# Token rows and gate products from bfloat16 thirds in place of fp32 matmuls

## The chip, the cores and the metric

One core of one Trainium2 chip. The metric is the device time of one execution in microseconds (us). A block is 128 tokens; most token chunks have four.

## The reference, cut to what matters

An input of 4 x 3072 x 256 goes through a two-dimensional Fourier transform (real part kept), a gated channel mix, and a mixture of 8 experts that gives every token to one expert as long as the expert has room.

```python
x = fft(fft(x, axis=1), axis=2).real                     # 4 x 3072 x 256
k = np.maximum(xk @ w_k, 0.0);  v = k * k @ w_v          # xk, xr: x mixed with the token before
r = 1.0 / (1.0 + np.exp(-(xr @ w_r)))
x = (r * v).reshape(12288, 256)                          # gated outputs, one row a token
logits = x @ w_gate                                      # 8 gate products a token
expert_idx = np.argmax(logits, axis=1)
...
# a token whose expert still has a free slot (384 each) goes through w1, relu, w2,
# times its softmax weight; all other rows of the output are zero
```

The choice of the expert is by the largest of eight products, so these are needed nearly exactly.

## The kernel before, in words

**Stages.** Up to 36 us: constants, weights cut into two fp32r halves, the first transform. From then to 470 us: token chunks of 512 (chunk 12 has 384, chunk 13 has 256). In this stage the Fourier transforms of the later inputs run as "units" placed between the matmuls of a chunk (`plan`, `lay`, L1047 to L1063). From 470 on: eight experts, each with two matmul stages, and the scatter of their results.

**A chunk (`chunk`, L647).** The channels lie on the 128 lanes and the tokens run along the free axis. Eight steps f: `mm_k` makes a hidden tile (six matmuls of 512 columns), ScalarE takes relu and square, `halves` (L538) lets VectorE cut it into two fp32r halves kh and kl, and `mm_v` uses them LAG = 3 steps later (six matmuls). So the last three `mm_v` of a chunk fall into the first three steps of the next one. In step 2 of chunk i the sums `pv` of chunk i - 1 are complete: `gated` (L556) multiplies them with the sigmoid on VectorE, into the tile rT, and the bank `pv` is free for `mm_v(i, 0)`. `mm_r(i)` follows (twelve matmuls). In steps 4 and 5 `to_rows` (L563) turns the gated outputs of chunk i - 1 into rows. For each block two matmuls, one per half of the 256 channels, have rT's block as the stationary operand and `gm` as the moving one: an identity of 128 columns with 8 gate columns beside it. They write 136 columns each, overlapping by 8, into 264 columns of one bank: 128 outputs, 8 gate products summed over both halves, 128 outputs. ScalarE copies them into `rows` (L576). One fp32 matmul runs as two passes, each with a weight load of its own.

**The choice.** `pick` (L578) finds the largest product on VectorE (L590 to L597) and leaves a one-hot tile `oh`. `route` (L600, step 6) counts tokens per expert with small bf16 matmuls on `oh` (L605, L609). `slots` and `place` make the slot numbers, `send` scatters the rows with an indirect transfer from GpSimd (L186) to `disp` in memory, whose row width is `RW`. The experts later read `disp` (`load_slots`, L1200) and turn rows back with `ident` (`turn`, L1217).

**The last chunk.** After chunk 13 `finish` (L693) does the same without a following chunk around it: `gated`, `to_rows`, `pick`, `route`, then `slots` and a flag which decides whether more blocks of tokens are needed. In this run they are not, so 14 chunks with 53 blocks are done.

**Order.** The schedule is manual: every engine executes in the order of the program text, and `later`/`tick` move a VectorE or ScalarE step behind the next matmul group. PSUM banks: three `pk` for hidden tiles, three `pm` for transforms, rows and routing, two `pv`. `gm` is filled by four transfers on SyncE's queue (L1016, L1017) at about 31 to 34 us, ahead of the loads of `w_v`; `ident` comes by ScalarE's queue (L930).

```python
if f == LAG - 1 and prev is not None:
    gated(prev)
if f == (LAG - 1 if i else LAG + 1):
    mm_r(i)
    tick()
```

Of the kernel before, what the change touches and what calls it, by code (L numbers as in the profile page):

```python
# [10 lines left out]
F32 = mybir.dt.float32  # L11
F32R = mybir.dt.float32r
BF16 = mybir.dt.bfloat16
I32 = mybir.dt.int32
AF = mybir.ActivationFunctionType
ALU = mybir.AluOpType
# [4 lines left out]
P = 128  # L21
# [11 lines left out]
CH = 512  # L33
# [6 lines left out]
GATE = 128  # L40
# [67 lines left out]
def fourier_channel_mix_moe(  # L108
# [6 lines left out]
    nc = tc.nc  # L115
    x = ins["x"]
    B, S, D = x.shape
    DFF = ins["w_k"].shape[1]
    E, _, F2 = ins["w1"].shape
    N = B * S  # L120
    KD = D // P
    KF = DFF // P
    KF2 = F2 // P
    RW = D + E + 1
    ST = cap // P
    NSLOT = E * cap
    TT = CH // P
    assert S == P * NC and D == 2 * P and cap % P == 0 and B == 4 and E == 8
    YC = (slice(0, P), slice(P + E, D + E))
    LC = slice(GATE, GATE + E)  # L130
    chunks = [(b, s, w) for b in range(B) for s, w in cut(b, S)]
    NCH = len(chunks)

    cst = ctx.enter_context(tc.tile_pool(name="cst", bufs=1))
# [3 lines left out]

    disp = drp.tile([NSLOT, RW], F32, name="disp")

    ident = cst.tile([P, P], F32, name="ident")
    flag = cst.tile([P, 1], I32, name="flag")
    slot = cst.tile([P, TT], I32, name="slot")
    rows_of = cst.tile([P, TT, RW], F32, name="rows")
    mix = ExitStack()
    psv = mix.enter_context(tc.tile_pool(name="psv", bufs=1, space=PSUM))
    wts = mix.enter_context(tc.tile_pool(name="wts", bufs=1))
# [3 lines left out]
    neg_i = wts.tile([P, P], F32R, name="neg_i")  # L151
    ulp_i, negulp_i = (wts.tile([P, P], BF16, name=f"ulp{k}") for k in range(2))
    ones = wts.tile([P, P], BF16, name="ones")
    gm = wts.tile([P, KD, P + E], F32, name="gm")
    w8 = wts.tile([P, TT, E], F32, name="w8")
    lim = wts.tile([P, TT, E], F32, name="lim")
    base = wts.tile([P, E], F32, name="base")
# [15 lines left out]
    mir = wts.tile([P, (len(CSTEPS) - 1) * B], I32, name="mir")  # L173
    blank = wts.tile([P, RW], F32, name="blank")

# [333 lines left out]
    live = {}  # L509
# [46 lines left out]
    def gated(i, step=None):  # L556
        rT, v = live[i, "r"], live.pop((i, "v"))
        w = chunks[i][2]
        for t in range(0, w, step or w):
            ts = slice(t, t + (step or w))  # L560
            nc.vector.tensor_tensor(rT[:, :, ts], v[:, :, ts], rT[:, :, ts], op=ALU.mult)  # L561

    def to_rows(i, ts):  # L563

        yT = live[i, "r"]
        if ts[0] == 0:
            live[i, "rows"] = early["rows"] if i == stop1 - 2 else rows_of
        rows = live[i, "rows"]
        for t in ts:
            ps = psm.tile([P, CH], F32, name="pm")  # L570
            for d in range(KD):
                nc.tensor.matmul(
                    ps[:, P * d:P * (d + 1) + E], yT[:, d, t * P:(t + 1) * P], gm[:, d],
                    start=(d == 0), stop=(d == KD - 1), skip_group_check=True,
                )
            nc.scalar.copy(rows[:, t, :D + E], ps[:, :D + E])  # L576

    def pick(i, clear=False):  # L578

        b, s, w = chunks[i]  # L580
        n = w // P
        rows = live[i, "rows"]
        nc.gpsimd.iota(
            rows[:, :n, RW - 1:].bitcast(I32), pattern=[[P, n], [0, 1]], base=b * S + s, channel_multiplier=1
        )
        if clear:
            nc.gpsimd.drain()
        lg = rows[:, :n, LC]
        mx = mp.tile([P, TT, 1], F32, name="mx")[:, :n]
        nc.vector.tensor_reduce(mx, lg, op=ALU.max, axis=AX.X)  # L590
        nc.vector.tensor_tensor(lg, lg, mx.to_broadcast([P, n, E]), op=ALU.subtract)
        key = mp.tile([P, TT, E], F32, name="key")[:, :n]
        nc.vector.scalar_tensor_tensor(key, lg, 0.0, w8[:, :n], op0=ALU.is_ge, op1=ALU.mult)
        mx2 = mp.tile([P, TT, 1], F32, name="mx2")[:, :n]
        nc.vector.tensor_reduce(mx2, key, op=ALU.max, axis=AX.X)
        oh = mp.tile([P, TT, E], BF16, name="oh")[:, :n]
        nc.vector.tensor_tensor(oh, key, mx2.to_broadcast([P, n, E]), op=ALU.is_equal)  # L597
        live[i, "oh"] = oh
# [48 lines left out]
    def chunk(i, prev, fill, nxt, mixes, also=()):  # L647


        also = dict(also)  # L650
        n = chunks[prev][2] // P if prev is not None else 0
        for f in range(KF):
            if f in also:
                also[f]()
            if f == 0 and (i, 1, 0) not in xm:
                mix_part(i, 0)
                mix_part(i, 1)
                settle()
            if f == (0 if i else 2) and (i, 0, 0) not in xm:
                for d in range(KD):  # L660
                    mix_part(i, 2 + d)
                if i and prev is None:
                    settle()
            mm_k(i, f)
            tick()
            if f >= LAG:
                mm_v(i, f - LAG)
                tick()
            elif prev is not None:
                mm_v(prev, KF - LAG + f)  # L670
                tick()
            if f == LAG - 1 and prev is not None:
                gated(prev)
            if f == (LAG - 1 if i else LAG + 1):
                mm_r(i)
                tick()
            if prev is not None:
                if f == LAG + 1:
                    to_rows(prev, range(0, min(2, n)))
                if f == LAG + 2:  # L680
                    if n > 2:
                        to_rows(prev, range(2, n))
                    later(1, lambda: pick(prev, True))
                if f == LAG + 3:
                    route(prev)
                    later(1, lambda: (slots(prev), place(prev), send(prev)))
            if nxt is not None and f in mixes:
                mix_part(nxt, mixes.index(f))
            for u in fill[f]:
                u()  # L690
                tick()

    def finish(i, before=lambda: None, between=lambda: None, after=lambda: None):  # L693
# [18 lines left out]
        "x": [[t.rearrange("p t s -> p (t s)")[:, cap * k:cap * (k + 1)] for t in fbuf["G"][0]] for k in range(KD)],  # L712
        "d": spare1[:, :ST * RW].rearrange("p (t w) -> p t w", w=RW),
        "rows": spare1[:, ST * RW:2 * ST * RW].rearrange("p (t w) -> p t w", w=RW),
        "count": spare1[:, 2 * ST * RW:2 * ST * RW + cap],
# [15 lines left out]
    def early_turn(k, last):  # L731
        ps = bank()
        for t in range(ST):
            nc.tensor.matmul(
                ps[:, t * P:(t + 1) * P], early["d"][:, t, YC[k]], ident, start=(t == 0),
                stop=(last and t == ST - 1), skip_group_check=True,
# [38 lines left out]
    def early_parts(i, step):  # L775
        for k, (h, l) in enumerate(early_room(i)[1]):
            v = live[i, "rows"][:, :h.shape[1], YC[k]]
            if step == 0:
# [116 lines left out]
    with tc.manual_schedule():  # L895
        with tc.tile_pool(name="stg", bufs=2) as stg:
# [116 lines left out]
            pw["r"][1]()  # L1013
            pw[0, 1][2]()
            for d in range(KD):
                nc.sync.dma_start(gm[:, d, P * (1 - d):P * (1 - d) + E], ins["w_gate"][d * P:(d + 1) * P])  # L1016
                nc.sync.dma_start(gm[:, d, E * d:E * d + P], ins["c_ident"])  # L1017
        mp = mix.enter_context(tc.tile_pool(name="mp", bufs=1))
        late_buffers(mp)
        vp = ExitStack()  # L1020
# [282 lines left out]
        for e in range(1, E + 1):  # L1303
            for f in range(KF2):
                if e < E:
                    up(e, f)
                t = f // 2 - 1 if e > 1 else f
# [43 lines left out]
```

## Time and profile before

| | |
|---|---|
| three timed runs | 622.03, 625.03, 629.35 us; median 625.03 |
| the profiled execution | 620.86 us, its span 619.1 us |
| mean granted TensorE clock | 0.989 |
| TensorE (PE) busy | 589.2 us, 95% of the span |
| VectorE (DVE) busy | 409.0 us, 66% |
| ScalarE (ACT) busy | 361.7 us, 58% |
| GpSimd (POOL) busy | 125.4 us, 20% |

Times in the rows are us from the start of the span unless marked ns. PE is a matmul, PEld a weight load, SPq the issue of a transfer on SyncE. [...] In a timeline a row merges equal instructions that follow each other (x8); brackets give the idle time of the engine before them and what ended it.

### The profile page before, as it was taken

How to read it: one execution, taken by the hardware profiler on the slowest of the kernel's cores; microseconds unless marked ns; L12 is line 12 of the kernel's file. 1: busy time of each engine (PE TensorE's matmuls, PEld its weight loads, DVE VectorE, ACT ScalarE, POOL GpSimd, SP SyncE). 2: the span in 40 equal slices, each digit the busy share in tenths (PEclk: the TensorE clock that was granted, in tenths of full speed). 3: DMA queues.
4: the chain of work that ended last, by engine and by line, in shares of the span. 5: the costliest groups of instructions: out<-in, count | busy, mean ns of one | idle time of the engine just before them, and what ended most of it. 6: DMA issues, size and time to landing. Idle time of an engine off the chain costs nothing. (4 is left out here: it accounts for less than half of the span.)

```text
span 619.1 us, 9641 instructions
## 1 busy us (share of the span) xinstructions
PE 589.2 (95%) x3365; PEld 506.7 (82%) x3367; DVE 409.0 (66%) x924; ACT 361.7 (58%) x710; POOL 125.4 (20%) x181
## 2 busy tenths in 40 slices
PE   6888988999999999999999999999997999999996
PEld 3474667888888788887888888889996999999996
DVE  5667896988665756799756565756764685665540
ACT  2556765666655566666655565565644675565551
POOL 7300052503020303050202030302221111111112
PEclk7999999999999999999999999999998999999999
DMA  8699342614242500152313052000023875555401
GB/s 275 228 341 318 127 152 86 215 43 138 54 144 76 166 0 22 34 187 87 126 46 104 14 186 89 6 2 3 3 63 92 303 214 162 177 152 163 124 26 35
DMA packets 55579, 74.02 MB, mean 120 GB/s; under 512 B 6288, under 2 KB 41469, under 8 KB 55522
## 3 DMA queue, kind: packets, MB, share of 16 engines
q1 hardware_dynamic: 48178, 58.35, 29.8%
q0 software_dynamic: 5936, 13.37, 6.5%
q10 hardware_dynamic: 1408, 1.60, 0.8%
q8 instruction: 29, 0.48, 0.3%
q14 instruction: 28, 0.23, 0.1%
HBM read 43.31 MB, written 33.91 MB: 125 GB/s over the span
## 5 line engine op out<-in xcount | busy, mean ns | idle before, releaser
L504 PE MATMUL pk<-x,wk 128*128 128x512 f32 (+2 forms) x672 | 171.1, 389 | 4.3 <-DVE x L218 1.7
L504 PEld LDWEIGHTS pk<-x,wk 128*128 128x128 f32 x672 | 118.7, 189 | 27.6 <-DVE x L218 2.6
L504 PE MATMUL pv<-kh,wv 128*128 128x512 f32 (+2 forms) x448 | 134.2, 381 | 2.3 <-DVE rT L561 1.4
L535 ACT ACTIVATE rk<-pk 128x512 f32<-128x512 f32 (+2 forms) x112 | 64.4, 575 | 85.0 <-PE pk L504 82.6
L186 POOL DMA_INDIRECT disp<-rows,slot x50 | 53.8, 1076 | 255.5 <-ACT tmp L494 64.4
L539 DVE CAST kh<-rk 128x512 fp32r<-128x512 f32 (+2 forms) x106 | 44.4, 419 | 85.9 <-ACT rk L536 85.5
L504 PEld LDWEIGHTS pv<-kh,wv 128*128 128x128 f32 x448 | 82.4, 188 | 19.8 <-DVE rT L561 2.3
L504 PE MATMUL pv<-kl,wv 128*128 128x512 f32 (+2 forms) x224 | 85.3, 381 | 0.0
L540 DVE TENSOR_TENSOR kl<-rk,kh 128x512 fp32r<-128x512 f32 (+2 forms) x112 | 74.5, 665 | 9.9 <-ACT kh L539 4.0
L1250 PE MATMUL pd<-w,h 128*128 128x256 f32 x576 | 72.5, 282 | 0.0
L1250 PEld LDWEIGHTS pd<-w,h 128*128 128x128 f32 x576 | 71.6, 191 | 0.0
L536 ACT ACTIVATE rk<-rk 128x512 f32<-128x512 f32 (+2 forms) x112 | 68.2, 609 | 3.6
L1198 DVE TENSOR_TENSOR w<-raw,w 128x512 fp32r<-128x512 f32 x60 | 41.0, 687 | 39.7 <-ACT w L1197 39.7
L504 PEld LDWEIGHTS pv<-kl,wv 128*128 128x128 f32 x224 | 42.1, 188 | 8.1
L186 POOL DMA_INDIRECT out<-res,ids x24 | 24.0, 998 | 117.5 <-ACT res L1259 117.2
L1241 DVE SCALAR_TENSOR_TENSOR h<-pk,h 128x384 fp32r<-128x384 f32 x64 | 35.3, 552 | 14.4 <-ACT h L1240 14.4
L1259 ACT ACTIVATE res<-pd,g 128x256 f32<-128x256 f32 x24 | 11.3, 476 | 53.6 <-PE pd L1250 52.1
L217 ACT CAST x<-tmp 128x512 fp32r<-128x512 f32 (+2 forms) x56 | 32.8, 587 | 14.2 <-DVE tmp L495 14.0
L504 PE MATMUL pk<-x,wr 128*128 128x512 f32 (+2 forms) x168 | 39.1, 382 | 0.0
L1197 ACT CAST w<-raw 128x512 fp32r<-128x512 f32 x60 | 36.6, 614 | 0.0
L218 DVE TENSOR_TENSOR x<-tmp,x 128x512 fp32r<-128x512 f32 (+2 forms) x56 | 36.5, 655 | 0.1
L504 PEld LDWEIGHTS pk<-x,wr 128*128 128x128 f32 x168 | 30.7, 188 | 6.3
(214 smaller groups left out, 861.6 us busy)
## 6 DMA issues: line engine op xcount, KB each, us to landing
raw<-in_w SPq DMA_DIRECT2D x60, 256.0 KB
out<-blank SPq DMA_DIRECT2D x24, 512.0 KB
xin<-in_x SPq DMA_DIRECT2D x15, 256.0 KB
tin<-fd SPq DMA_DIRECT2D x18, 208.0 KB
fd<-f SPq DMA_DIRECT2D x14, 256.0 KB
disp<-blank SPq DMA_DIRECT2D x6, 530.0 KB
d<-disp SPq DMA_DIRECT2D x8, 397.5 KB
rawv<-in_w_v SPq DMA_DIRECT2D x4, 512.0 KB
```

The source lines that it names most:

```text
L186: i = nc.gpsimd.indirect_dma_start(out=dst, out_offset=bass.IndirectOffsetOnAxis(ap=idx, axis=0), in_=src, in_offset=None, bounds_check=la ...
L217: nc.scalar.copy(hl[0], src)
L218: later(n, lambda: nc.vector.tensor_tensor(hl[1], src, hl[0].bitcast(F32), op=ALU.subtract))
L504: nc.tensor.matmul(ps, w[a][:, k, m0:m0 + P], xs[c], start=(first and n == 0), stop=(last and n == 2),)
L535: nc.scalar.activation(r, ps, AF.Relu)
L536: nc.scalar.activation(r, r, AF.Square)
L539: nc.vector.tensor_copy(kh, r) if i or f > 5 else nc.scalar.copy(kh, r)
L540: nc.vector.tensor_tensor(kl, r, kh.bitcast(F32), op=ALU.subtract)
L1197: nc.scalar.copy(h, r)
L1198: nc.vector.tensor_tensor(l, r, h.bitcast(F32), op=ALU.subtract)
L1241: nc.vector.scalar_tensor_tensor(hl, ps, 0.0, hh.bitcast(F32), op0=ALU.max, op1=ALU.subtract)
L1250: nc.tensor.matmul(ps, hs[a][:, f, t * P:(t + 1) * P], w[c][:, f], start=(f == 0 and n == 0), stop=(f == KF2 - 1 and n == 2),)
```

## The change

`thirds` cuts the gated output y of a chunk into three bf16 parts that add up to it exactly: the upper half word of y, the upper half word of the rest r, and what is then left. `gm` becomes bf16 and holds the gate weights cut in the same way, beside the identity. Each block and half gets one matmul per part of y in place of one fp32 matmul. The first part meets three parts of the gate weights (24 columns beside the identity), the second two, the third one, so the products stand in three groups of 8 columns, and `pick` adds these up. The moving operand is `gm`; the stationary ones are the parts of y, each spaced by one half word in an fp32 tile. `finish` doesn't call `thirds`: there the fp32 `gw`, whose added 16 columns are zero, is used as before, with 152 columns. `RW` grows from 265 to 281. `ident` is now a part of `gw`. The parts of the gate weights are made on GpSimd, once.

```diff
--- before.py
+++ after.py
@@ -121,12 +121,12 @@
     KD = D // P
     KF = DFF // P
     KF2 = F2 // P
-    RW = D + E + 1
+    RW = D + 3 * E + 1
     ST = cap // P
     NSLOT = E * cap
     TT = CH // P
     assert S == P * NC and D == 2 * P and cap % P == 0 and B == 4 and E == 8
-    YC = (slice(0, P), slice(P + E, D + E))
+    YC = (slice(0, P), slice(P + 3 * E, D + 3 * E))
     LC = slice(GATE, GATE + E)
     chunks = [(b, s, w) for b in range(B) for s, w in cut(b, S)]
     NCH = len(chunks)
@@ -138,7 +138,8 @@
 
     disp = drp.tile([NSLOT, RW], F32, name="disp")
 
-    ident = cst.tile([P, P], F32, name="ident")
+    gw = cst.tile([P, KD, P + 3 * E], F32, name="gw")
+    ident = gw[:, 0, :P]
     flag = cst.tile([P, 1], I32, name="flag")
     slot = cst.tile([P, TT], I32, name="slot")
     rows_of = cst.tile([P, TT, RW], F32, name="rows")
@@ -151,7 +152,8 @@
     neg_i = wts.tile([P, P], F32R, name="neg_i")
     ulp_i, negulp_i = (wts.tile([P, P], BF16, name=f"ulp{k}") for k in range(2))
     ones = wts.tile([P, P], BF16, name="ones")
-    gm = wts.tile([P, KD, P + E], F32, name="gm")
+    gm = wts.tile([P, KD, P + 3 * E], BF16, name="gm")
+    gf = wts.tile([P, KD, E], F32, name="gf")
     w8 = wts.tile([P, TT, E], F32, name="w8")
     lim = wts.tile([P, TT, E], F32, name="lim")
     base = wts.tile([P, E], F32, name="base")
@@ -560,20 +562,35 @@
             ts = slice(t, t + (step or w))
             nc.vector.tensor_tensor(rT[:, :, ts], v[:, :, ts], rT[:, :, ts], op=ALU.mult)
 
+    def upper(t):
+        return t.bitcast(BF16)[..., 1::2]
+
+    def thirds(i):
+        w = chunks[i][2]
+        y = live[i, "r"]
+        r = mp.tile([P, KD, CH], F32, name="yr")[:, :, :w]
+        low = r.bitcast(BF16)[..., 0::2]
+        nc.vector.tensor_tensor(r, y, upper(y), op=ALU.subtract)
+        nc.vector.tensor_tensor(low, r, upper(r), op=ALU.subtract)
+        live[i, "y"] = [upper(y), upper(r), low]
+
     def to_rows(i, ts):
 
-        yT = live[i, "r"]
+        ys = live.pop((i, "y")) if ts[-1] == chunks[i][2] // P - 1 and (i, "y") in live else live.get((i, "y"))
+        ys = [(live[i, "r"], gw)] if ys is None else [(y, gm) for y in ys]
         if ts[0] == 0:
             live[i, "rows"] = early["rows"] if i == stop1 - 2 else rows_of
         rows = live[i, "rows"]
         for t in ts:
             ps = psm.tile([P, CH], F32, name="pm")
             for d in range(KD):
-                nc.tensor.matmul(
-                    ps[:, P * d:P * (d + 1) + E], yT[:, d, t * P:(t + 1) * P], gm[:, d],
-                    start=(d == 0), stop=(d == KD - 1), skip_group_check=True,
-                )
-            nc.scalar.copy(rows[:, t, :D + E], ps[:, :D + E])
+                for k, (y, g) in enumerate(ys):
+                    c = slice(E * k, P + 3 * E) if d else slice(0, P + E * (3 - k))
+                    nc.tensor.matmul(
+                        ps[:, P * d + c.start:P * d + c.stop], y[:, d, t * P:(t + 1) * P], g[:, d, c],
+                        start=(d == k == 0), stop=(d == KD - 1 and k == len(ys) - 1), skip_group_check=True,
+                    )
+            nc.scalar.copy(rows[:, t, :RW - 1], ps[:, :RW - 1])
 
     def pick(i, clear=False):
 
@@ -586,6 +603,8 @@
         if clear:
             nc.gpsimd.drain()
         lg = rows[:, :n, LC]
+        for k in (1, 2):
+            nc.vector.tensor_tensor(lg, lg, rows[:, :n, GATE + E * k:GATE + E * (k + 1)], op=ALU.add)
         mx = mp.tile([P, TT, 1], F32, name="mx")[:, :n]
         nc.vector.tensor_reduce(mx, lg, op=ALU.max, axis=AX.X)
         nc.vector.tensor_tensor(lg, lg, mx.to_broadcast([P, n, E]), op=ALU.subtract)
@@ -671,6 +690,7 @@
                 tick()
             if f == LAG - 1 and prev is not None:
                 gated(prev)
+                thirds(prev)
             if f == (LAG - 1 if i else LAG + 1):
                 mm_r(i)
                 tick()
@@ -1013,8 +1033,18 @@
             pw["r"][1]()
             pw[0, 1][2]()
             for d in range(KD):
-                nc.sync.dma_start(gm[:, d, P * (1 - d):P * (1 - d) + E], ins["w_gate"][d * P:(d + 1) * P])
-                nc.sync.dma_start(gm[:, d, E * d:E * d + P], ins["c_ident"])
+                nc.gpsimd.memset(gw[:, d, P * (1 - d):P * (1 - d) + 3 * E], 0.0)
+                for g in (gw[:, d, P * (1 - d):P * (1 - d) + E], gf[:, d]):
+                    nc.sync.dma_start(g, ins["w_gate"][d * P:(d + 1) * P])
+                if d:
+                    nc.sync.dma_start(gw[:, d, 3 * E:], ins["c_ident"])
+                nc.gpsimd.tensor_copy(gm[:, d, 3 * E * d:3 * E * d + P], ident)
+            for k in range(3):
+                for d in range(KD):
+                    g = gm[:, d, E * (2 - k):E * (3 - k)] if d else gm[:, d, P + E * k:P + E * (k + 1)]
+                    nc.gpsimd.tensor_copy(g, upper(gf[:, d]))
+                    if k < 2:
+                        nc.gpsimd.tensor_tensor(gf[:, d], gf[:, d], upper(gf[:, d]), op=ALU.subtract)
         mp = mix.enter_context(tc.tile_pool(name="mp", bufs=1))
         late_buffers(mp)
         vp = ExitStack()
```

## Rows read from the trace of the kernel before

**Rows 1.** The page, part 1: busy us (share of the span) xinstructions, whole run
```profile
PE 589.2 (95%) x3365; PEld 506.7 (82%) x3367; DVE 409.0 (66%) x924; ACT 361.7 (58%) x710; POOL 125.4 (20%) x181
```

**Rows 2.** Busy us by stretches (xinstructions); then granted clock, DMA share, GB/s
```profile
97.00:125.00 28.00, 26.18 (x136) 21.32 (x135) 25.56 (x53) 17.09 (x33) 8.91 (x10) 1.00 0.45 147
246.00:276.00 30.00, 29.73 (x154) 24.66 (x153) 24.60 (x52) 19.61 (x36) 9.22 (x10) 1.00 0.29 95
276.00:306.00 30.00, 28.75 (x155) 23.99 (x154) 26.79 (x58) 19.57 (x35) 6.83 (x7) 1.00 0.38 128
366.00:396.00 30.00, 30.00 (x163) 25.16 (x162) 17.87 (x46) 18.25 (x36) 3.94 (x5) 1.00 0.33 107
```

**Rows 3.** Groups by line and shape: line 572 (busy us, mean ns, idle before)
```profile
L572 PE MATMUL pm<-gm,rT 128*128 128x136 f32 x212 | 29.2, 279 | 0.8 <-ACT rows L576 0.8
```

**Rows 4.** Timeline, TensorE near 287: start us, us, engine, line, operation
```profile
287.61 1.09 PE L572 MATMUL pm<-gm,rT 128*128 128x136 f32 x8
```

**Rows 5.** Timeline and line 609: short, contiguous and spaced matmuls
```profile
23.36 1.06 PE L837 MATMUL pk<-raw,ulp 128*128 128x512 bf16 x2
24.24 0.83 PE L887 MATMUL pk<-busy 128*128 128x512 bf16 x3
26.88 0.40 PE L887 MATMUL pk<-busy 128*128 128x512 bf16 x1 [0.27 <-issue]
...
107.10 0.39 PE L609 MATMUL pm<-oh,ones 128*128 128x8 bf16 x10
L609 PE MATMUL pm<-oh,ones x129: 166/166/167, 107.1 to 463.8; 128*128 128x8 bf16 x129
...
449.98 0.87 PE L504 MATMUL pk<-x,wk 128*128 128x256 f32 x6
450.68 0.28 PE L504 MATMUL pv<-kh,wv 128*128 128x256 f32 x1
```

**Rows 6.** Line 312: duration ns min/median/max, first and last start, forms
```profile
L312 DVE TENSOR_TENSOR xin<-xin x14: 425/692/711, 8.2 to 299.6; 128x512 f32<-128x512 f32 x12, 128x256 f32<-128x256 f32 x2
```

**Rows 7.** Timeline, VectorE and TensorE from 281 to 296
```profile
281.37 1.22 DVE L561 TENSOR_TENSOR rT<-pv,rT 128x1024 f32<-128x1024 f32 x1
...
287.73 0.43 DVE L539 CAST kh<-rk 128x512 fp32r<-128x512 f32 x1 [0.35 <-ACT rk L536]
...
293.97 0.18 DVE L590 TENSOR_REDUCE mx<-rows 128x4 f32<-128x32 f32 x1
...
294.86 0.19 DVE L597 TENSOR_TENSOR oh<-key,mx 128x32 bf16<-128x32 f32 x1
295.72 0.19 PE L605 MATMUL pm<-oh,tri 128*128 128x32 bf16 x1
```

**Rows 8.** Timeline, VectorE and TensorE from 447 to 456
```profile
447.92 0.95 DVE L561 TENSOR_TENSOR rT<-pv,rT 128x768 f32<-128x768 f32 x1
451.39 1.09 PE L572 MATMUL pm<-gm,rT 128*128 128x136 f32 x8
...
455.66 0.18 DVE L597 TENSOR_TENSOR oh<-key,mx 128x24 bf16<-128x24 f32 x1
455.90 0.19 PE L605 MATMUL pm<-oh,tri 128*128 128x24 bf16 x1 [0.18 <-ACT rk L536]
```

**Rows 9.** Timeline, chunk 1: VectorE near 98, TensorE near 107
```profile
97.69 0.69 DVE L311 TENSOR_TENSOR dif<-xin 128x512 f32<-128x512 f32 x1 [4.45 <-DMA xin<-in_x,mir]
...
107.07 0.19 PE L605 MATMUL pm<-oh,tri 128*128 128x32 bf16 x1 [0.83 <-DVE oh L597]
```

**Rows 10.** Timeline, VectorE and TensorE near 263
```profile
263.23 0.19 DVE L597 TENSOR_TENSOR oh<-key,mx 128x32 bf16<-128x32 f32 x1
263.76 0.19 PE L605 MATMUL pm<-oh,tri 128*128 128x32 bf16 x1
```

**Rows 11.** Waits (us, times, longest) and line 1016: GpSimd's idle, SyncE's issues
```profile
POOL wk L178 <- DVE x L218: 52.9, 1, 52.9
L1016 SPq DMA_DIRECT2D gm<-in_w_gate x2: 328/328/328, 31.2 to 33.2; - x2
```

## The prediction

> **What bounds the kernel now.** I read the busy shares of the page first, then busy time and granted clock by stretches, then the gated-output matmuls and the waits around them in order of time. TensorE is busy for 95% of the span, VectorE for 66%, ScalarE for 58%, GpSimd for 20% [rows 1]. [...] The chain that ended last helps little: its long pieces lie in the expert stage, which the change hardly touches.
>
> **The matmuls.** Line 572 has 212 records: 53 token blocks, two halves each, two passes for an fp32 matmul, each 0.279 us long by its record [rows 3]. Eight of them take 1.09 us, so one starts (1.09 - 0.28) / 7 = 0.116 us after another, and a block costs 4 x 0.116 = 0.463 us [rows 4]. Of the 53 blocks 51 are done inside the chunk loop, where thirds() runs; the last chunk's two go through finish(), which has no thirds, and stay fp32. A changed block has six bf16 matmuls of 152, 144 and 136 columns, twice: 864 columns and six weight loads.
>
> What these cost isn't in the trace; rows bound it. Contiguous bf16 matmuls of 512 columns start 0.215 us apart (three take 0.83, one alone 0.40), 0.42 ns a column; by columns alone a block costs 864 x 0.42 = 0.363 us [rows 5]. Ten bf16 pairs of load and 8-column matmul take 0.39 with a last one of 0.166, 0.025 us a pair: a load of 128 bf16 weights takes that or less [rows 5]. A straight line from 0.025 at 8 columns to 0.215 at 512 gives 0.076 at 144, 0.458 a block, no gain to speak of. Six pairs of 256 columns with a new weight each run from 449.98 to 450.68, 0.117 apiece, 0.009 above 256 x 0.42 [rows 5]; those 9 ns six times on top of 0.363 give 0.42. I take the middle of 0.363 and 0.42, 0.392, since these rows have pairs of the nearest kind: 0.071 saved a block, 51 x 0.071 = 3.6 us. The far end is a weight load that is no faster than an fp32 one; then a pair costs what it does now, at most 0.116, and six 0.695: 0.232 more a block, 11.8 us in all. What speaks for that end: the new weights are every second half word of an fp32 tile. The nearest row has a moving operand at every fourth half word: two such matmuls take 1.06 us where three contiguous ones take 0.83 [rows 5], about twice as long each. A load of 0.025 that doubled would still hide behind 0.06 of columns, so I stay with 0.392 and keep the far end for the range.
>
> [...]
>
> **thirds() on VectorE.** Two subtractions over 1024 elements a lane, directly behind the gating product. That product has the same shape and takes 1.22 us [rows 7]; twice 512 elements from SBUF would be 2 x 0.69 [rows 6], so one lies between 1.22 and 1.38. I take 2.45 us a chunk for both, 1.9 for the 384-wide one. They don't hold up their own consumer: from the product at 281.37 to the first row matmul at 287.61 there are 6.24 us, in the narrow last chunk from 447.92 to 451.39 3.47; the thirds are ready after 1.22 + 2.45 = 3.7 and 0.95 + 1.9 = 2.85 [rows 4, 7, 8]. Queued behind them on VectorE is later work: halves of hidden tiles, mixes of the next chunk, folds, and in the end the choice of the expert. In chunk 1 the push falls into a wait of 4.45 us for a transfer [rows 9]. In quiet chunks it is gone in a few us, because VectorE waits for ScalarE there. In the chunk from 281.37 VectorE has just 0.35 us of idle before the choice at 293.97 [rows 7], so some 2.1 us of the 2.45 are still there.
>
> **Two small sums in pick().** 32 elements a lane, like the chain from 293.97 to 294.86, four steps of 0.22 [rows 7]: 0.44 us, 14 times, always in front of the choice for which the routing matmuls wait. What it costs depends on the slack there, the more so as TensorE now comes 4 x 0.071 = 0.28 us earlier.
> At 107.07 TensorE waits 0.83 for VectorE already [rows 9]: 0.44 more and the 0.28 lost, 0.72.
> At 263.76 the choice ended at 263.42 [rows 10], slack 0.34: 0.44 + 0.28 - 0.34 = 0.38.
> At 295.72 it ended at 295.05, slack 0.67 [rows 7]: 2.1 + 0.44 + 0.28 - 0.67 = 2.15.
> At 455.90 it ended at 455.84, slack 0.06 [rows 8]: 0.44 + 0.21 - 0.06 = 0.59.
> In finish() routing waits for the choice in any case: 0.44, and eight fp32 passes with 152 for 136 columns, 0.11: 0.55.
> I allow 0.3 for the other chunks. Together 4.7 us; as little as 0.55 if VectorE finds idle time ahead of these places that I don't count.
>
> **What stays hidden.** ScalarE copies 280 for 264 columns, a hundredth of a us. GpSimd gets 14 small operations at the start and has one wait of 52.9 us in that stage [rows 11]. SyncE gets one issue more before the loads of w_v, where issues are 1 us apart (the two of w_gate, with another between, at 31.2 and 33.2) [rows 11]: 0 to 1 us; I take 0, as that stage also waits for the weights' conversions. Dispatch rows grow by 6%, over transfer engines busy for 29 to 45% in these stretches [rows 2].
>
> **Sum.** -3.6 + 4.7 = +1.1 us. The profiled execution took 620.86 us (its span of 619.1 and 1.8 around it), less than any of the three timed runs (622.03 to 629.35); it would become 622.0, and I carry the difference to their median: 625.03 + 1.1 = 626.1 us.
>
> **Rivals.**
> The gain arrives whole (18%): the row matmuls cost their columns, 51 x 0.100 = 5.1, and only finish() gives 0.55 back: 620.5. For it: VectorE is 60% busy in a quiet stretch, from 366 to 396 [rows 2]. Against it: the waits at 107 and 295.
> Short pairs don't hide in each other (12%): 0.458 a block, a gain of 0.3; with TensorE no earlier the waits come to 0.44 + 0.1 + 1.87 + 0.38 + 0.55 = 3.3, so +3, 628.1. Against it: the pairs of 256 columns.
> The spaced loads are slow (12%): +11.8 us. TensorE is then 0.93 us later in each chunk, which covers all waits but 2.54 - 0.67 - 0.93 = 0.9 at 295 and the 0.55: +13.3, 638. It is the clear case on the slower side, and TensorE loses from the point where one pair takes over 0.463 / 6 = 0.077 us. For it: the spaced moving operand. Against it: the 0.025 us pairs.
> VectorE becomes the bound where it is fullest (10%): its idle time there can't be used, and 2.45 + 0.44 show in each of four chunks, 11.6; less 3.6 and with 0.55 that is +8.6, 633.6. For it: 91% busy from 97 to 125. Against it: the 4.45 us it waits in chunk 1, and LAG: a hidden tile's halves are due three tiles later.
> My forecast has the other 48%; by itself 623 to 629.5.
>
> **How the numbers follow.** A measurement of this kernel tells about 1% from no change: 618.8 to 631.3. Faster than that needs the whole gain and some luck, 0.07. Slower: the slow loads, most of the VectorE case, a tail of the short pairs, 0.22. Within: 0.71. Below 620 lies a third of the first rival (6%), above 634.5 the slow loads (12%): the range is 620 to 634.5.
>
> **What would show it.** Right: six matmuls a block 0.06 to 0.07 us apart where four stood at 0.116; two VectorE subtractions of some 1.2 us behind each gating product; a wait of 1.5 to 2.5 us at the routing matmul near 295; VectorE busier by 12 x 2.45 + 1.9 + 14 x 0.44, some 37 us, at 72% of the span. Wrong: pairs of 0.1 us or more; no longer wait near 295; row matmuls that wait for the thirds themselves.

## The result and the profile after

The changed kernel took 628.24 us (median of 6 runs, 627.85 to 629.46) where the kernel before took 623.40 on the same chip: a ratio of 1.0079 [1.0054, 1.0105], some 4.9 us more. The forecast was 1.1 us more, and within 1%. So the sign and the range held, and the amount did not: 3.8 us are to be found. The forecast of 626.1 us had 625.03 for the kernel before, which is 623.40 in the larger set of runs, so the absolute time looks closer than the difference is.

The profiled execution took 627.94 us, its span 626.1, at a mean granted clock of 0.985 (0.989 before). The page's part 1, answering to [rows 1]:

```profile
PE 593.4 (95%) x3467; PEld 504.2 (81%) x3469; DVE 445.7 (71%) x978; ACT 361.7 (58%) x710; POOL 128.1 (20%) x195
```

VectorE is busy 36.7 us longer, as forecast. TensorE is not busy for less: 593.4 us against 589.2. The stretches of [rows 2] again, with the same columns:

```profile
97.00:125.00 28.00, 26.16 (x139) 21.05 (x138) 23.84 (x53) 15.97 (x30) 10.39 (x12) 0.94 0.48 157
246.00:276.00 30.00, 29.34 (x155) 23.45 (x154) 25.92 (x54) 19.97 (x35) 8.61 (x10) 1.00 0.22 68
276.00:306.00 30.00, 27.90 (x152) 22.52 (x151) 27.64 (x58) 17.59 (x32) 4.81 (x6) 0.94 0.37 122
366.00:396.00 30.00, 30.00 (x173) 24.77 (x173) 20.76 (x47) 17.30 (x37) 4.91 (x5) 1.00 0.44 142
```

From 366 to 396 TensorE is as full as before, 30.00 of 30 us. In two of the three stretches with folds the granted clock is 0.94 instead of 1.00, and from 276 to 306 TensorE stands still for 0.85 us more. Now the groups by line and shape: the new matmuls, the two subtractions (lines 573 and 574) and the sums (607):

```profile
L589 PE MATMUL pm<-gm,rT 128*128 128x152 bf16 x102 | 20.6, 232 | 1.8 <-ACT rows L593 1.8
L589 PE MATMUL pm<-gm,yr 128*128 128x144 bf16 x102 | 20.2, 226 | 0.0
L589 PE MATMUL pm<-gm,yr 128*128 128x136 bf16 x102 | 20.1, 223 | 0.0
...
L574 DVE TENSOR_TENSOR yr<-yr 128x1024 bf16<-128x1024 f32 x12 | 16.7, 1393 | 0.4
L573 DVE TENSOR_TENSOR yr<-rT 128x1024 f32<-128x1024 f32 x12 | 14.7, 1225 | 0.4
...
L607 DVE TENSOR_TENSOR rows<-rows 128x32 f32<-128x32 f32 x24 | 4.6, 191 | 1.3
```

**Chunk 1, where the first microsecond is lost.** The timeline of the changed kernel, GpSimd, VectorE, ScalarE and TensorE from 92 to 105:

```profile
92.62 1.23 DVE L573 TENSOR_TENSOR yr<-rT 128x1024 f32<-128x1024 f32 x1
...
93.28 1.44 POOL L180 DMA_INDIRECT wr<-flip,neg  x1 [0.30 <-issue]
93.88 1.40 DVE L574 TENSOR_TENSOR yr<-yr 128x1024 bf16<-128x1024 f32 x1
...
95.03 2.03 POOL L289 DMA_INDIRECT xin<-in_x,mir  x1 [0.30 <-issue]
95.17 0.68 DVE L220 TENSOR_TENSOR x<-tmp,x 128x512 fp32r<-128x512 f32 x1
...
99.44 0.69 DVE L313 TENSOR_TENSOR dif<-xin 128x512 f32<-128x512 f32 x1 [2.80 <-DMA xin<-in_x,mir]
...
103.53 0.62 ACT L219 CAST x<-tmp 128x512 fp32r<-128x512 f32 x1 [4.97 <-DVE tmp L497]
104.05 0.68 ACT L593 COPY rows<-pm 128x280 f32<-128x280 f32 x2
104.49 0.23 PE L589 MATMUL pm<-gm,rT 128*128 128x152 bf16 x1 [1.84 <-ACT rows L593]
104.83 2.49 PE L506 MATMUL pk<-x,wk 128*128 128x512 f32 x6
```

And the same place before the change:

```profile
92.61 1.06 POOL L178 DMA_INDIRECT wr<-flip,neg  x1 [0.30 <-issue]
93.97 1.00 POOL L287 DMA_INDIRECT xin<-in_x,mir  x1 [0.30 <-issue]
...
102.74 0.73 PE L572 MATMUL pm<-gm,rT 128*128 128x136 f32 x4 [0.81 <-ACT rows L576]
```

The fold of the next transform waits for a gathering DMA that GpSimd issues. While the subtractions and the mix behind them run, one issue takes 1.44 us where it took 1.06, and the next 2.03 where it took 1.00: 1.4 us. The fold starts at 99.44 instead of 97.69 [rows 9], of which 0.74 is there already at the chunk's twelve `pk<-x,wr` (90.12 and 89.38, below); 1.0 us remains. What stands behind the fold on VectorE is late with it, ScalarE waits 4.97 us for it instead of the 4.08 of before, its copies of the rows are late in turn, and TensorE waits 1.84 us instead of 0.81 for a free row buffer. Then the granted clock falls from 1.00 to 0.50, and at a second such place to 0.51, by stretches:

```profile
105.30:108.70 3.40, 3.40 (x10) 2.64 (x9) 2.61 (x8) 3.34 (x7) 0.00 (x0) 0.50 0.25 80
286.20:289.60 3.40, 3.40 (x12) 2.91 (x11) 3.33 (x5) 0.25 (x1) 0.00 (x0) 0.51 0.02 5
```

Six 512-column matmuls behind the wait take 2.49 us (104.83) where six at a granted clock of 1.00 take 1.56 (92.91). At the second place, chunk 7, TensorE's waits are these, both in the changed kernel:

```profile
285.88 0.95 PE L506 MATMUL pv<-kh,wv 128*128 128x512 f32 x2 [1.90 <-DVE rT L563]
...
300.69 0.19 PE L624 MATMUL pm<-oh,tri 128*128 128x32 bf16 x1 [0.20 <-DVE oh L616]
```

The wait was forecast at the second of them, for the choice, and comes at the first, for the gating product: before, TensorE waited there too, 1.25 us. TensorE then runs at a granted clock of 0.51 from 286.20 to 289.60, and VectorE, busy for 3.33 of these 3.40 us, catches up meanwhile. Why the first wait is 1.90 here and 1.21 in layout (below), no run shows.

**All long matmuls are a little slower.** Twelve 512-column matmuls of chunk 1 that stand behind one another, before and after the change, by the timeline:

```profile
89.38 2.91 PE L504 MATMUL pk<-x,wr 128*128 128x512 f32 x12
```

```profile
90.12 2.95 PE L506 MATMUL pk<-x,wr 128*128 128x512 f32 x12
```

A record lasts longer than the distance to the next start. With some 0.4 for the last of them, (2.91 - 0.39) / 11 = 229 ns from one to the next before and (2.95 - 0.40) / 11 = 232 ns after. Nothing of the change touches these instructions. The gap is there in all chunks of the plain weights (0 to 2 and 6 to 8: means of 229.0 to 230.5 ns before and 232.2 to 232.9 after, each from one chunk's `pk<-x,wr` to the next) and, at 0.4 to 1.6 ns, smaller in the others. Over the whole chunk stage, two neighbouring 512-column matmuls start 230.8 ns apart on the mean before and 232.8 after.

### The profile page after: what moved, and what is told of

Read it like the earlier page. It is cut to its first block, busy times and chain, and to the rows that moved or that the text cites. A ratio compares the mean times of both kernels' runs of the same rounds, so it can differ in the third digit from the quotient of the medians.

```text
span 626.1 us, 9907 instructions
## 1 busy us (share of the span) xinstructions
PE 593.4 (95%) x3467; PEld 504.2 (81%) x3469; DVE 445.7 (71%) x978; ACT 361.7 (58%) x710; POOL 128.1 (20%) x195
## 5 line engine op out<-in xcount | busy, mean ns | idle before, releaser
L506 PE MATMUL pv<-kh,wv 128*128 128x512 f32 (+2 forms) x448 | 136.6, 386 | 2.6 <-DVE rT L563 1.9
```

The source lines that it names most:

```text
L506: nc.tensor.matmul(ps, w[a][:, k, m0:m0 + P], xs[c], start=(first and n == 0), stop=(last and n == 2),)
```

## The experiments

Ratios are to the kernel before on the same chip, from five rounds. The stage column is the length of the chunk stage in one profiled execution: from the first start to the last of the matmuls pv<-kh,wv, by their line. For the kernel before and the changed one the rows are

```profile
L504 PE MATMUL pv<-kh,wv x448: 276/392/505, 61.4 to 459.5; 128*128 128x512 f32 x128, 128*128 128x384 f32 x11, 128*128 128x256 f32 x11
```

```profile
L506 PE MATMUL pv<-kh,wv x448: 279/393/632, 62.0 to 464.7; 128*128 128x512 f32 x128, 128*128 128x384 f32 x11, 128*128 128x256 f32 x11
```

that is 398.1 and 402.7 us: 4.6 us lie in this stage. (The spans of the two profiled executions differ by more than the medians do, 7.0 us: 0.6 ahead of the stage and 1.8 behind it, where 161.4 us follow in the changed kernel, 159.6 before, 160.4 in layout and quiet_sums, and 159.5 in quiet, which has no sums in `finish`.) What lies ahead of it can't be judged by one profile: the first start is 61.4 in the kernel before and 63.9 in before_pad, which has the same instructions.

| kernel | median us | ratio [interval] | stage us |
|---|---|---|---|
| before, profiled run | 620.86 | | 398.1 |
| changed | 628.24 | 1.0079 [1.0054, 1.0105] | 402.7 |
| neither | 628.40 | 1.0123 [1.0089, 1.0158] | 404.3 |
| thirds_only | 630.33 | 1.0134 [1.0109, 1.0159] | 406.6 |
| bf_only | 623.83 | 1.0025 [1.0007, 1.0044] | 399.1 |
| before_pad | 622.94 | 1.0012 [0.9990, 1.0034] | 398.1 |
| before_pad64 | 624.41 | 1.0024 [1.0002, 1.0046] | 400.5 |
| layout | 626.30 | 1.0045 [1.0024, 1.0066] | 400.3 |
| no_sums | 871.38 | 1.3999 [1.3953, 1.4044] | not comparable |
| quiet | 621.04 | 0.9973 [0.9954, 0.9991] | 396.7 |
| quiet_sums | 623.05 | 1.0003 [0.9986, 1.0020] | 398.1 |
| quiet_wide | 623.17 | 1.0017 [0.9997, 1.0036] | 398.8 |
| sums_twice | 631.50 | 1.0144 [1.0112, 1.0177] | 405.6 |

**Subtractions and matmuls apart.** Three kernels on the changed one. neither leaves out the subtractions and keeps fp32 matmuls, with the wider weights (152 columns):

```
-        nc.vector.tensor_tensor(r, y, upper(y), op=ALU.subtract)
-        nc.vector.tensor_tensor(low, r, upper(r), op=ALU.subtract)
-        live[i, "y"] = [upper(y), upper(r), low]
```

> The changed kernel without its two subtractions on VectorE; all blocks are turned by the fp32 matmuls of 152 columns (before: 136), the sums in the choice of the expert and the wider rows stay. If the subtractions make the loss (theory A), the two long waits of TensorE near 104 and 286 us and the two drops of the granted clock behind them are gone, and the time is that of before plus 53 blocks x 4 x 0.014 us = 3.0 for the wider matmuls and 1 to 1.5 for the sums: +4 to +4.5 us. If the sums make it (theory B), the waits near 266 and 300 and in the last chunk stay and the time is +5 or more with the waits near 104 and 286 still there. If all matmuls of the chunk stage got slower because their tiles moved in SBUF (theory C), the distance of two 512-column matmuls is 232.7 ns as in the changed kernel, against 230.8 before, and 3 us come on top: +7 to +7.5.

thirds_only makes the subtractions and uses fp32 matmuls all the same:

```
-        ys = [(live[i, "r"], gw)] if ys is None else [(y, gm) for y in ys]
+        ys = [(live[i, "r"], gw)]
```

> The two subtractions run as in the change, but their result isn't used: all blocks are turned by the fp32 matmuls of 152 columns. Theory A: the cost of the subtractions alone is the difference to the kernel without them, +3 to +5 us, with the waits near 104 and 286 and both drops of the clock. Theory B: under 1 us.

bf_only has the bf16 matmuls without subtractions, three times on the upper third, so that its rows hold the upper third three times over and nothing of the two lower ones:

```
-        nc.vector.tensor_tensor(r, y, upper(y), op=ALU.subtract)
-        nc.vector.tensor_tensor(low, r, upper(r), op=ALU.subtract)
-        live[i, "y"] = [upper(y), upper(r), low]
+        live[i, "y"] = [upper(y)] * 3
```

> Three bf16 matmuls per block and half, but on the upper third of the outputs three times over (the output is not exact: the two lower thirds are left out), with no subtractions on VectorE. Against the kernel with neither part: a block takes 0.407 us in place of 4 x 0.129 = 0.516, 51 x 0.109 = 5.6 us faster. Against before: theory A, under 0 (the 2.5 us that the changed trace shows as gain, less 1 to 1.5 for the sums); theory C, +1.5 to +2, with 512-column matmuls at 232.7 ns; theory B, +3 or more.

The kernel called neither fits theories A and C together (some 7.7 us by its ratio, no fall of the clock, its mean 0.989 as before, a wait of 1.0 us near 103 for 1.84), bf_only fits theory C. thirds_only is in part a miss: its waits are there (1.42 us near 104, 1.35 at the choice in chunk 7), but its execution has no fall of the clock in the stage (its mean is 0.996), where two were expected.

By the stage, the subtractions cost 406.6 - 404.3 = 2.3 us beside fp32 matmuls and 402.7 - 399.1 = 3.6 beside bf16 ones. The bf16 matmuls save 5.2 and 3.9 us against fp32 ones of 152 columns, which are themselves dearer than the 136 of before (records of 293 ns in `finish` of the changed kernel, for 279). These are differences of single executions: the ratios of neither and thirds_only, 1.0123 and 1.0134, have intervals too wide to show the 2.3 us. And something is left that none of the three edits takes away: bf_only ends up 1.0 us behind the kernel before although its matmuls are faster and only the small sums are added. All three have the long matmuls of the changed kernel (2.96 us for the twelve of chunk 1 in thirds_only and bf_only; the means of all three are below).

**Where tiles lie.** What all of them share is the table of tiles. Two kernels on the one before: before_pad moves everything behind ident by 544 bytes a lane, before_pad64 makes the gap behind blank 64 bytes larger, by as much as the rows grow; no instruction is changed.

```
     ident = cst.tile([P, P], F32, name="ident")
+    cst.tile([P, 136], F32, name="pad")
```

> The kernel before with 544 unused bytes a lane behind the identity, which moves all later tiles of the chunk stage by as much as the change moves them. Theory C: 512-column matmuls at 232.7 ns in place of 230.8, +3 us. Otherwise no difference.

```
     blank = wts.tile([P, RW], F32, name="blank")
+    wts.tile([P, 16], F32, name="pad")
```

> The kernel before with 64 unused bytes a lane behind the weights and ahead of the tiles of the mixed inputs and hidden halves: in the changed kernel the wider blank row moves these by as much against the weights. Theory C2 (the distance in SBUF between a matmul's weights and its moving operand sets its speed): the 512-column matmuls of chunks 0 to 2 and 6 to 8 rise from 229.5 to some 232.5 ns apart, and the time by about 3 us. If the slower matmuls of the change come from elsewhere (more work on VectorE, the new order), no difference.

The first does nothing (398.1 us in the stage, as before): moving the tiles as such is not the cause. The second lengthens the stage by 2.4 us, and its twelve matmuls of chunk 1 take what they take in the changed kernel:

```profile
89.78 2.95 PE L505 MATMUL pk<-x,wr 128*128 128x512 f32 x12
```

So half of the loss has nothing to do with matmuls of thirds: blank is 16 numbers longer, and with it the distance between the weights of the long matmuls and their moving tiles. The counterpart, layout, is the changed kernel with the distances of before:

```
+    mir = wts.tile([P, (len(CSTEPS) - 1) * B], I32, name="mir")
     d1 = [wts.tile([P, 2 * P], F32R, name=f"d1{h}") for h in range(2)]
...
-    mir = wts.tile([P, (len(CSTEPS) - 1) * B], I32, name="mir")
     blank = wts.tile([P, RW], F32, name="blank")
+    wts.tile([P, 8], F32, name="pad")
```

> The changed kernel with one small index tile moved ahead of the weights and 32 bytes of padding behind them, so that the weights and the moving operands lie as far apart as in the kernel before; no instruction differs. Theory C2: 512-column matmuls back at 230.8 ns on the mean, 3 us faster than the change, before +2. Theory A and B alone: the time of the change, before +5.

The group of twelve is back, and the stage is 2.4 us shorter than the changed kernel's:

```profile
94.17 2.91 PE L507 MATMUL pk<-x,wr 128*128 128x512 f32 x12
```

The ratios alone, 1.0045 and 1.0079, have intervals that just overlap; the matmuls settle it. Their mean distance in the stage is 230.8 to 231.0 ns in before, before_pad, layout, quiet, quiet_sums and sums_twice, and 232.7 or 232.8 in the changed kernel, neither, thirds_only, bf_only, before_pad64 and quiet_wide.

The waits of TensorE in layout (us in total, times, longest) for the choice, which the prediction had named, and for a free row buffer, which it had not; they were 1.1 and 0.8 us before:

```profile
PE pm L625 <- DVE oh L617: 5.0, 5, 1.8
...
PE pm L590 <- ACT rows L594: 2.0, 1, 2.0
```

**The sums.** no_sums leaves the two sums out of the choice:

> The changed kernel without the two sums in the choice of the expert, which then goes by the first group of products alone (the lower parts of the products are left out). Theory B, as the prediction had it: 0.44 us at each place where routing waits for the choice, 1.5 to 2 us in all, before +3. If the subtractions make the loss, under 1 us.

A miss, and not the edit that was meant. The gate weights of the second half of the channels stand in `gm` in the opposite order, so the first group of 8 columns holds the main products of the first 128 channels and only the smallest part of those of the other 128, whose main part is in the third group. So the choice went by one half of the channels, more work was asked for by the kernel's own flag, and the time of 871.38 us (448 of those matmuls became 640) says nothing on the cost of a sum.

**Leaving the fullest chunks alone.** quiet is layout, with fp32 matmuls and no subtractions for the three chunks whose work on VectorE meets the folds, and with sums only where there are thirds:

```
     def thirds(i):
+        cutup.add(i)
...
-        for k in (1, 2):
+        for k in (1, 2) if i in cutup else ():
...
-                thirds(prev)
+                if prev not in (0, 5, 6):
+                    thirds(prev)
```

> The layout kernel with the subtractions and the sums left out in chunks 0, 5 and 6, whose rows are made where VectorE is fullest, and the sums left out in the last chunk; those chunks use the fp32 matmuls of 152 columns. Theory A: the long waits near 104 and 286 and the drops of the clock go, 3 to 4 us less than the layout kernel, before -1 to -2. Theory C2 without A: within 1 us of the layout kernel.

It is faster than either kernel: 0.9973, and 1.0003 for quiet_sums, which has the sums in front of every choice again:

```
-        for k in (1, 2) if i in cutup else ():
+        for k in (1, 2):
```

> As the version called quiet (no subtractions for chunks 0, 5 and 6, whose rows stay fp32; weight distances as before), but the two small sums stand in front of every choice again, those of chunks 0, 5, 6 and of the finish too. Theory, as on record: a sum pair is 0.44 us and shows wherever the routing matmul already waits for the choice: at the finish and behind chunks 0, 5 and 6, so some 1 to 1.8 us over quiet, a ratio to the kernel before of 0.999 to 1.001. Rival: the sums find slack everywhere but at the finish: 0.44 us, 0.998. Other rival: the subtractions alone made the difference and the sums cost nothing: 0.997.

The difference, 0.0030 or 1.9 us, is at the upper end of what the theory gave for the sums of three chunks and the finish; the rivals (0.44 us, or nothing) would be ratios of 0.998 and 0.997, and both lie outside its interval; but quiet has an interval of its own, and against that the smaller rival isn't ruled out (the stage alone says 1.4 us, and quiet's execution had a fall of the clock in it, see The clock). From quiet_sums to layout, 0.0042 or 2.6 us (2.2 in the stage), is the cost of the subtractions in three chunks, after what the faster matmuls of these give back: from one chunk's `pk<-x,wr` to the next, layout is 1.85 us longer than quiet_sums in chunk 7 and 0.44 in chunk 1. GpSimd's first gathering issue of this place takes 1.01 us in quiet_sums (1.43 in quiet, 1.01 in bf_only, 2.02 or 2.03 in the four kernels with subtractions in chunk 0).

quiet_wide is quiet with the tiles where the change puts them:

> The changed kernel with the subtractions and sums left out for chunks 0, 5 and 6 and the sums left out at the finish, but the tiles where the change puts them, so the weights of the long fp32 matmuls lie 64 bytes further from their moving tiles than before. Theory: the distance costs the same whatever else is in the kernel, 229.5 to 232.5 ns for each of the 512-column matmuls of chunks 0 to 2 and 6 to 8, 2.0 to 3.0 us in all, so a ratio to the kernel before of 1.0005 to 1.002 where quiet gave 0.997. Rival: the distance only matters where VectorE's subtractions collide with it, then it is gone with them and the ratio is that of quiet, 0.997.

1.0017 against 0.9973: 2.7 us, 2.1 in the stage. The distance costs the same without the subtractions. The theory holds, and its rival is outside the interval.

**The sums counted twice**, on layout:

```
             nc.vector.tensor_tensor(lg, lg, rows[:, :n, GATE + E * k:GATE + E * (k + 1)], op=ALU.add)
+            nc.vector.tensor_tensor(lg, lg, lg, op=ALU.max)
```

> The version called layout (all subtractions and sums, weight distances as before) with two further operations of the same size on VectorE in front of each choice, that leave the values as they are, so the sums' cost counts twice. Theory: the choice is late at the routing matmuls behind chunks 0, 5, 6 and 12 and at the finish, 0.44 us each: 1.3 to 2.6 us over layout, a ratio to the kernel before of 1.0065 to 1.009. Rival: the waits are set by the transfer in chunk 1 and by the gating product, not by the choice: 0.44 us at the finish alone, 1.005.

Both were wrong: 6.2 us over layout, 5.3 of them in the stage. The largest piece is in chunk 7, shown here in layout and in sums_twice:

```profile
303.42 0.19 PE L625 MATMUL pm<-oh,tri 128*128 128x32 bf16 x1 [1.84 <-DVE oh L617]
...
303.71 0.96 PE L353 MATMUL pm<-xsp,d 128*128 128x258 f32 x6
304.50 1.55 PE L507 MATMUL pk<-x,wk 128*128 128x512 f32 x6
```

```profile
301.07 0.19 PE L626 MATMUL pm<-oh,tri 128*128 128x32 bf16 x1 [2.29 <-DVE oh L618]
...
301.36 1.63 PE L353 MATMUL pm<-xsp,d 128*128 128x258 f32 x6
302.79 2.45 PE L507 MATMUL pk<-x,wk 128*128 128x512 f32 x6
```

The wait grows by 0.45, the price of the added operations. But behind 2.29 us of standing still the clock falls in this execution (a mean of 0.78 from 298 to 304 where layout has 1.00), and the next twelve matmuls take 1.63 + 2.45 instead of 0.96 + 1.55: by starts, 301.36 to 305.08 against 303.71 to 305.89, 1.54 us more. Together that is 2.0 us; that the longer wait brought the fall is not shown, as falls also follow shorter waits (see The clock). Ahead of it, chunk 7 loses another 0.8 us at the gating product (a wait of 2.04 for 1.21), and six other places lose 0.3 to 0.5 us each, as the theory has it.

## Why the prediction was right in its range and short in its amount

**The matmuls: right in kind, the size off.** Six matmuls stand 0.06 us apart as forecast, and no load of their weights, every second half word, shows: twelve from 98.49 to 99.22, with loads whose records last 98 ns, where those of the fp32 matmuls of before last 190. Here are two blocks with the six long matmuls behind them, before and after:

```profile
97.62 1.09 PE L572 MATMUL pm<-gm,rT 128*128 128x136 f32 x8
...
98.46 1.64 PE L504 MATMUL pk<-x,wk 128*128 128x512 f32 x6
...
99.93 0.62 PE L504 MATMUL pv<-kh,wv 128*128 128x512 f32 x2
```

```profile
98.49 0.24 PE L589 MATMUL pm<-gm,rT 128*128 128x152 bf16 x1
98.57 0.28 PE L589 MATMUL pm<-gm,yr 128*128 128x144 bf16 x2
...
99.13 0.28 PE L589 MATMUL pm<-gm,yr 128*128 128x144 bf16 x2
99.22 1.63 PE L506 MATMUL pk<-x,wk 128*128 128x512 f32 x6
...
100.69 0.63 PE L506 MATMUL pv<-kh,wv 128*128 128x512 f32 x2
```

0.84 us became 0.73, 0.365 a block; with the six behind them 2.31 became 2.20. So a pair of blocks saves 0.11, and 51 blocks 2.8 us; layout, from one chunk's `pk<-x,wr` to the next, is 0.21 to 0.25 us shorter than before in the eight chunks without longer waits (2 to 5 and 8 to 11). The term said 3.6: it had taken 0.463 for a block of before, from the distance of its passes, but the next matmul starts closer behind the last pass, and two blocks cost 0.84 there, not 0.93. The value for the new block, 0.392, was if anything too high. The 0.365 us of six such pairs agree with 0.363 by columns alone, and twelve pairs at 136 to 152 columns start 0.73 / 12 = 61 ns apart.

**The subtractions: right, a little short.** 1.23 and 1.39 us make 2.62 a chunk for a forecast of 2.45. VectorE's sum came out at 36.7 us for 37. They never hold up their own row matmuls: the one wait of TensorE at line 589 is that of 1.84 us for the rows.

**The waits at the choice: right in size, with layout as the judge,** which has the distances of before. By the starts of the same matmuls in both timelines it loses 1.60 us in chunk 1 (forecast 0.72), 0.67 in chunk 6 (0.38), 2.02 in chunk 7 (2.15) and 0.44 in the last (0.59): 4.7, where the forecast had 3.8 for these four. Less the 2.8 this leaves 1.9 of the 2.2 us that layout's stage is longer. At the choice itself the four lose 0.60, 0.37, 2.0 and 0.44, 3.4 us; the other 1.3 are 1.0 at the rows of chunk 1 and 0.3 at a transform matmul of chunk 6, which the forecast had not. Its sign, a wait of 1.5 to 2.5 us at the choice near 295, is there in layout (1.84) and not in the changed kernel's execution (0.20), where the wait ahead of it and the fall of the clock came in its place.

**Chunk 1: the step that failed.** "In chunk 1 the push falls into a wait of 4.45 us for a transfer": it did so in part only. VectorE's idle time there shrank from 4.45 to 2.80 us, and the transfer itself came later: its issue on GpSimd ran beside the subtractions and took 2.03 us for 1.00. From the chunk's first `pk<-x,wr` to the fold it is 8.31 us before and 9.22 to 9.34 in the four kernels with subtractions in chunk 0; in the six others, quiet left out because its clock had just fallen, it is 8.09 to 8.86, so part of the 1.0 us can be the spread of the transfer. TensorE's wait for the rows is 1.42 to 2.02 us with the subtractions and 0.63 to 1.11 without. The reading took a wait for a transfer as a buffer of fixed end, without asking who starts the transfer.

**What the sum did not have: where the tiles lie.** 2.1 to 2.7 us by three comparisons (before_pad64's stage, layout and the changed kernel, quiet and quiet_wide), half of the loss. The prediction counted the rows' 6% as bytes to transfer only. With it the sum is -2.8 + 4.7 + 2.4 = 4.3 of the 4.6 us in the stage. The 0.55 of `finish` lies behind the stage, where the profiles can't tell it from their spread. That 628.24 us still fell into the forecast's own 623 to 629.5 is luck in part: this term was not in the sum for which that band was made.

**The clock.** The forecast treated each wait as its own length. In chunk 7 of sums_twice a longer wait came with a fall, and cost its own length and 1.5 us of slow matmuls. In the changed kernel the two falls come in chunks 1 and 7, and from one chunk's `pk<-x,wr` to the next these lose 1.6 and 2.6 us in all, against 1.5 and 1.8 in layout, which has no fall there: so most of the slow time took the place of a wait that would have followed. What decides whether the clock falls stays open, and the length of the wait alone is not it: in chunk 1 a wait of 1.84 us was followed by a fall in the changed kernel, one of 2.02 by none in layout. At the start of chunk 1 the same wait is followed by a fall in quiet, and by none in quiet_sums, layout and the kernel before. First quiet, the wait and then a stretch with the columns of [rows 2]:

```profile
81.07 0.50 PE L507 MATMUL pk<-x,wk 128*128 128x512 f32 x1 [1.76 <-DVE x L221]
82.30:85.70 3.40, 3.40 (x9) 2.63 (x9) 3.29 (x6) 1.79 (x3) 2.50 (x3) 0.51 0.66 199
```

and quiet_sums:

```profile
83.15 0.50 PE L507 MATMUL pk<-x,wk 128*128 128x512 f32 x1 [1.75 <-DVE x L221]
84.40:87.80 3.40, 3.40 (x16) 2.82 (x15) 3.30 (x6) 3.10 (x6) 2.53 (x3) 1.00 0.64 181
```

In quiet the fall costs 1.6 us up to the chunk's `pk<-x,wr`, and from there to the next chunk's it is 1.8 us shorter than before, because the waits of chunk 1 are gone. So a fall seen in one execution is no fixed part of the price of a change.

**The rivals.** None took place as a whole. The gain arrives whole only where VectorE has room (0.21 to 0.25 us a chunk in layout, for the 0.22 of two pairs of blocks), and quiet, which stays away from the other chunks and has the tiles where they were, comes out 0.3% faster than before; quiet_wide, without the second, does not (1.0017). VectorE as the bound is what chunk 7 shows, for 2 us and in one chunk where that rival had four.

## What to carry to other kernels

Here work that was moved from the bound engine to the second one paid in the chunks where the second had room and cost in the others (a ratio of 1.0045 for layout, 0.9973 for quiet): split the loop by that, as quiet does, before giving up the change. When a tile that lies between others changes its size, compare instructions that the change does not touch; here a difference of 1% in them (232 for 229 ns) was a matter of layout and could be mended by itself. And ask of each wait for a transfer which engine issues it and whether that issue takes longer beside the work that is added, as one here took 2.03 us for 1.00.

## What was not expected of the hardware

**The distance of operands.** 64 bytes more between the weights and the moving tiles of 512-column fp32r matmuls made each 232 instead of 229 ns, with the same instructions and the same data (before_pad64). 544 bytes in front of both did nothing (before_pad: the twelve of chunk 1 take 2.91 us, as before). A rival is left: by the edits the moving tiles lie 0, 544 and 640 bytes further on than before in the kernels with 229 ns (before, before_pad, layout), and 608 and 64 in those with 232 (the changed one, before_pad64). No run moves the weights alone, so it may be the place of the moving tiles and not the distance. Which places are bad wasn't tried any further.

**GpSimd's issue beside VectorE.** In chunk 1 the issue of a gathering DMA took 1.00 us before the change and 2.03 beside the end of the second subtraction and the mix behind it. In quiet, which has no subtractions there, the rows are:

```profile
91.06 1.05 POOL L181 DMA_INDIRECT wr<-flip,neg  x1 [0.30 <-issue]
91.15 1.22 DVE L564 TENSOR_TENSOR rT<-pv,rT 128x1024 f32<-128x1024 f32 x1
92.28 0.68 DVE L221 TENSOR_TENSOR x<-tmp,x 128x512 fp32r<-128x512 f32 x1
92.41 1.43 POOL L290 DMA_INDIRECT xin<-in_x,mir  x1 [0.30 <-issue]
```

Beside the product with one operand in PSUM an issue took 1.05, and one that begins beside the mix of two SBUF tiles took 1.43. The subtractions of the change are of the second kind. But in the kernel before an issue took 1.00 although a subtraction of two SBUF tiles runs beside most of it, from just behind its start:

```profile
89.99 1.00 POOL L178 DMA_INDIRECT wr<-flip,neg  x1 [0.30 <-issue]
90.03 0.69 DVE L540 TENSOR_TENSOR kl<-rk,kh 128x512 fp32r<-128x512 f32 x1
```

So the kind of instruction does not settle it alone. Whether it matters where the inputs lie, or that VectorE is busy as such, no run isolates.
